# An attention stage ordered by a list planner for five engines, instead of a hand-written slot table for TensorE

## The chip, the cores and the metric

The kernel runs on one core of a Trainium2 chip. The metric is the device time of one execution in microseconds (us). Three executions of the kernel before gave 1341.52, 1343.77 and 1346.31 us; the median is 1343.77.

Five engines work side by side, each through its own instructions in order: TensorE (PE, with its weight loads as PEld), VectorE (DVE), ScalarE (ACT), GpSimd (POOL) and SyncE (SP), which here only issues DMAs.

## The reference

Causal attention over blocks of 64 tokens, and behind it a bilinear feed-forward network (FFN). Eight batches of eight heads, 576 tokens, head size 64; FFN from 512 to 1536 and back to 512, everything in float32.

```python
scores = scale * np.matmul(q, k.transpose(0, 1, 3, 2))        # (8, 8, 576, 576)
mask = block_i >= block_j                                     # blocks of 64 tokens
scores = np.where(mask, scores, -1000000000.0)
scores = scores - np.max(scores, axis=-1, keepdims=True)
attn = np.exp(scores)
attn = attn / (np.sum(attn, axis=-1, keepdims=True) + 1e-09)
x = np.matmul(attn, v)                                        # then heads side by side: (4608, 512)
out = (x @ w_a) * (x @ w_b) @ w_out                           # w_a, w_b: (512, 1536), w_out: (1536, 512)
```

## The kernel before

The 64 heads are taken as 32 pairs, four pairs to a batch. The 12 blocks of 128 FFN columns are cut in two: the first pass computes four of them (F1 = 4) while attention runs, and the two later passes, after attention, compute the other eight. float32 products are made of three products of split halves (hi·hi, hi·lo, lo·hi); the first six pairs (NATIVE) do their scores in plain float32 instead.

For one pair the attention stage does this, on the engines named:

- **Scores** (PE, L384): five tiles of 128 queries, called by their number: tile 3 (512 keys), the side tile 4 (128 keys: the first and the last block of queries), tile 1 (320 keys), then tile 2 (448) and tile 0 (192). Each head has its own PSUM bank; the pool `ps_sc` holds six banks, `ps_mm` two.
- **Maxima** (DVE, `nm`, L389), with memsets for the mask (L395, L407, L408); `nb` joins the maxima of tile 3 and the side tile.
- **Exponentials** (ACT, `e`, L392), and the sums of rows with them; `rc` (DVE) is one over the sums.
- **Normalization** (POOL, L439): every `e` times its `rc`, in place, ten instructions.
- **Transposition** (DVE, L453 and L458): 32x32 blocks of `e` into the buffer `bl`, and then sixteen DMAs from SP (L463, `at<-bl`) which carry the 4x4 block matrix to its transposed places in `at`. There is one `at` (ATB = 1) and one `bl`.
- **Values** (PE, L477, `av`): 60 matmuls of `v` with `at`. They need all sixteen DMAs, and the next pair's sixteen DMAs must wait for them, since `at` is single.
- **x**: ACT copies `av` to `xf`, splits it to `xh` (ACT) and `xl` (POOL), and issues the DMA `xd<-xf` from its own queue.

The first pass of the FFN runs in between on PE (L223, products of 12 matmuls with 288 columns each). After the first product of a block, ACT copies it out (`a`, L247); DVE multiplies the second with it (`hf`, L249); ACT and POOL split that into `hh` and `hl`; the third product (`pso`) is copied by ACT to `ob` and stored by SP. Its weights come from HBM as 64-bit floats and are converted by DVE and ACT (`convert_w`, 12 parts).

The order of the work is fixed on PE alone. A table, SLOT, is walked once per slot (33 slots); in slot s it takes the steps of the softmax of pair s, the transposition of pair s-1 and the values of pair s-1, and after each step it lets as many matmuls of the first pass run as the column of numbers says:

```python
SLOT = [(*S1, 8), (*T1, 0), (*S1, 8), (*T1, 0), (*T1, 0), (*S1, 8), (*T1, 0), (*T1, 0), (*S1, 8),
        (*T1, 0), (*T1, 0), (*T1, 0), (*T1, 0), (*S1, 9), (*S1, 9), (*S1, 9), (*S1, 13), (V_, -1, 0)]
```

Once the first pass has begun, one slot holds 30 score matmuls, 72 of the first pass on average, and 60 value matmuls. On the other engines the framework's scheduler orders the instructions. `keep` matmuls, on zeros, fill PE in the first slots.

After attention the rest of the first pass (336 matmuls with 288 columns), the conversion of the other weights and the two later passes follow (L685, L731).

Of the kernel before, what the change touches and what calls it, by code (L numbers as in the profile page):

```python
# [8 lines left out]
F32 = mybir.dt.float32  # L9
# [11 lines left out]
CONV_POOL = 1  # L21
CONV_POOL2 = 0
CONV_PER_SLOT = 0.88
CONV0 = 1
HL_DVE = False
MOE_FROM = 10.2
FR = 6
X_EVERY = 48
OB = 3
PQ = lambda nc: nc.sync  # L30
XQ = lambda nc: nc.scalar
PE_ORDER = ["PE"]
WARM = 9
ATB = 1
KEEP = [3, 1, 1, 1, 1]
NATIVE = 6

XFB = 2
MORE = 6
PREF = True  # L40
# [4 lines left out]
LATE = 1  # L45
LO2 = lambda nc: nc.vector
CONVP = [1]*12
TLS = False
BEHIND = 5
NOSYNC = mybir.DependencyInfo(mybir.DependencyClass.NoSync, mybir.DependencyReason.DATA)  # L50
CONV_EVERY = 12
# [3 lines left out]
def attention_then_bilinear_ffn(  # L55
# [46 lines left out]
    ps_mm = psum(ctx, "ps_mm", 2)  # L102
# [111 lines left out]
    marks = []  # L214
    lo_eng = [nc.gpsimd]

    def mm3(ps, sets):

        n = 3 * len(sets)
        i = 0  # L220
        for wh, wl, dh, dl in sets:
            for w_, d_ in ((wh, dh), (wh, dl), (wl, dh)):
                mm = nc.tensor.matmul(ps, w_, d_, start=(i == 0), stop=(i == n - 1))  # L223
                if i == 0 and len(marks) > BEHIND:
                    tc.add_manual_dep(mm.ins, marks[-1 - BEHIND].ins.name, NOSYNC, reason="not ahead of attention")
                i += 1
                yield
# [40 lines left out]
    ps_sc = psum(right, "ps_sc", 6)  # L268
# [14 lines left out]
    SIDE, SIDE_T = 3, 1  # L283
    QB = 32
    NQ = P // QB
    NE = 4
    e_bufs, s_bufs = [], []
    for i in range(NE):
        es = [const.tile([P, ew[t]], F32, name=f"e{i}_{t}") for t in range(NT)]
        for t in range(LAST):  # L290
            nc.gpsimd.memset(es[t][:, nk[t]:], 0.0)
        e_bufs.append((es, const.tile([P, P], F32, name=f"e{i}_s")))
    at_e = [sum(ew[:t]) // P for t in range(NT)]
    NE_ = sum(ew) // P + 1
    bl = const.tile([P, NQ, 2, NE_, QB], F32, name="bl")
    nc.gpsimd.memset(bl[:, :, :, NE_ - 1], 0.0)
# [9 lines left out]
    if WARM:  # L306
        z = const.tile([P, W], F32R, name="z")
# [6 lines left out]
    xs_all = {}  # L314

# [13 lines left out]
    def load_qk(p):  # L329

        b, h, n = pair_of(p)
        take(p, "k", S, kT[b, h:h + 2].rearrange("h d s -> (h d) s"))
        take(p, "q", SQ, qT[b, h:h + 2].rearrange("h d s -> (h d) s"))

    def load_v(p):
        b, h, n = pair_of(p)
        vv = heads[p]["v"] = apool.tile([P, 2, NCH + 1, D], F32, tag="v", name=f"v{n}", bufs=3)
        nc.sync.dma_start(vv, vm[b, h // 2])

    def parts_of(p, tag):  # L340
        return heads[p].pop(f"{tag}r"), *(heads[p][tag].bitcast(F32R)[:, j] for j in (1, 0))

    def split_qk(p):
        if p < NATIVE:
            qq = heads[p]["q"]
# [533 lines left out]
```

## Time and profile before

| | |
|---|---|
| median of three executions | 1343.77 us |
| profiled execution: its own time, its span | 1344.45 us, 1342.7 us |
| mean granted PE clock | 0.917 |
| PE busy | 1170.9 us (87%) |
| DVE busy | 907.5 us (68%) |
| ACT busy | 531.3 us (40%) |
| POOL busy | 344.9 us (26%) |
| first score matmul, last value matmul | 5.7 us, 735.6 us |

In lines of the profile, a group reads "line engine operation out<-in shape xcount"; what stands in square brackets is the time the engine was idle just before, and who released it. In the list of waits the three numbers are the total in us, the number of waits and the longest. In the table of windows each engine has its busy time in us and its instructions in brackets; then come the granted PE clock as a share of full speed, the busy share of the DMA engines, and GB/s. SPq is SP's queue of DMA issues.

### The profile page before, as it was taken

Reading aid. Unit: us, or ns where it says so; the run is one execution under the profiler, and the core shown is the slowest. Engines: PE = TensorE matmul, PEld = TensorE weight load, DVE = VectorE, ACT = ScalarE, POOL = GpSimd, SP = SyncE. Lnnn points to the kernel's source line nnn. Section 1 sums busy time; section 2 is a strip of 40 time slices with the busy share of each in tenths; the row PEclk is TensorE's granted clock in tenths of the full one; section 3 lists DMA queues with packets and bytes.
Section 4 is the critical chain, followed back from the end, with each engine's and each line's share of the span. In section 5 each row is a group of like instructions: output and inputs, shape, how many; then the busy total and the mean of one; then the engine's idle time right before and its main releaser. Section 6 shows DMA issues by size and latency. Waiting matters only on the chain.

```text
span 1342.7 us, 23315 instructions
## 1 busy us (share of the span) xinstructions
PE 1170.9 (87%) x8357; PEld 1103.8 (82%) x8357; DVE 907.5 (68%) x2254; ACT 531.3 (40%) x1390; POOL 344.9 (26%) x537
## 2 busy tenths in 40 slices
PE   6466787878787878787877999999999999999998
PEld 3345687768687867686777999999999999999998
DVE  6978656564656465646564998977887876677664
ACT  3435354444444444444443554433433422122110
POOL 2343544444444444444432002102201200000000
PEclk8676988889888889888888999999999999999999
DMA  5666565555555655565545446446628931442231
GB/s 182 185 178 177 156 181 150 143 153 164 148 143 152 164 148 142 154 166 149 139 127 128 159 128 157 123 114 153 159 82 264 304 100 54 130 142 70 73 94 60
DMA packets 88629, 194.50 MB, mean 145 GB/s; under 512 B 15296, under 2 KB 41920, under 8 KB 88512
## 3 DMA queue, kind: packets, MB, share of 16 engines
q1 hardware_dynamic: 76992, 174.12, 45.3%
q0 software_dynamic: 6912, 9.44, 4.4%
q10 hardware_dynamic: 4608, 9.44, 1.9%
q8 instruction: 66, 1.08, 0.4%
q14 instruction: 51, 0.42, 0.1%
HBM read 87.03 MB, written 47.19 MB: 100 GB/s over the span
## 4 chain that ended last, share of the span: by engine, by line
PE 47%; DVE 19%; issue 10%; ACT 9%; POOL 9%; DMA 3%; SPq 2%; DVEq 0%; POOLq 0%; ACTq 0%
PE pso_z L731 14%; DVE bl L453 9%; PE psv_z L685 7%; PE psx_z L685 7%; PE psw_z L685 7%; ACT e L392 6%; DVE nm L389 6%; POOL e L439 4%; PE psy_z L685 3%; PE s L384 3%; PE ps L223 3%; POOL k L115 3%; PE pso L223 3%; DMA v<-vm 2%; SPq L463 1%
## 5 line engine op out<-in xcount | busy, mean ns | idle before, releaser
L223 PE MATMUL ps<-xh,wab 128*128 128x288 f32 x1024 | 233.7, 315 | 49.3 <-ACT a L247 40.9
L223 PEld LDWEIGHTS ps<-xh,wab 128*128 128x128 f32 x1024 | 178.3, 200 | 62.3 <-ACT a L247 45.4
L731 PE MATMUL pso_z<-h_z,wo 128*128 128x384 f32 x1152 | 203.3, 334 | 0.0
L731 PEld LDWEIGHTS pso_z<-h_z,wo 128*128 128x128 f32 x1152 | 200.0, 188 | 0.4 <-ACT h_z L112 0.3
L223 PE MATMUL pso<-hh,wo 128*128 128x288 f32 x480 | 117.3, 334 | 54.7 <-ACT a L247 49.6
L223 PE MATMUL ps<-xl,wab 128*128 128x288 f32 x512 | 159.3, 311 | 3.4 <-POOL xl L115 3.1
L384 PE MATMUL s<-k,q 64*128 64x512 f32 (+3 forms) x900 | 126.2, 416 | 33.4 <-ACT e L392 27.3
L439 POOL TENSOR_SCALAR e<-e,rc 128x512 f32<-128x512 f32 (+3 forms) x256 | 145.4, 586 | 36.8 <-DVE rc L435 36.8
L389 DVE TENSOR_REDUCE nm<-s 128x1 f32<-128x512 f32 (+4 forms) x320 | 142.4, 475 | 3.4 <-PE s L384 1.4
L384 PEld LDWEIGHTS s<-k,q 64*128 64x128 f32 x900 | 91.9, 234 | 61.2 <-ACT e L392 33.7
L223 PEld LDWEIGHTS pso<-hh,wo 128*128 128x128 f32 x480 | 89.9, 216 | 61.1 <-ACT a L247 52.4
L453 DVE STREAM_TRANSPOSE bl<-e 128x512 f32<-128x512 f32 (+2 forms) x256 | 130.5, 575 | 0.9 <-POOL e L439 0.4
L477 PEld LDWEIGHTS av<-at,v 128*64 128x64 f32 x1920 | 102.0, 149 | 31.4 <-issue 19.0
L477 PE MATMUL av<-at,v 128*64 128x128 f32 (+1 forms) x1920 | 106.3, 274 | 24.0 <-DMA at<-bl 22.6
L392 ACT ACTIVATE e<-s,nm 128x448 f32<-128x448 f32 (+2 forms) x192 | 100.1, 533 | 55.1 <-DVE nm L389 54.6
L794 POOL DMA_DIRECT2D part<-pt x48 | 42.7, 1070 | 299.3 <-ACT pt L793 299.3
L112 ACT CAST h_z<-u_z 128x384 fp32r<-128x384 f32 x96 | 49.3, 514 | 176.2 <-DVE u_z L710 160.3
L685 PE MATMUL psw_z<-xh,wab 128*128 128x384 f32 x384 | 116.2, 338 | 0.0
L458 DVE STREAM_TRANSPOSE bl<-e_s 64x64 f32<-64x64 f32 x128 | 27.2, 230 | 131.7 <-POOL e_s L439 123.1
L685 PE MATMUL psv_z<-xh,wab 128*128 128x384 f32 x384 | 116.1, 337 | 0.0
L685 PE MATMUL psx_z<-xh,wab 128*128 128x384 f32 x384 | 116.0, 338 | 0.0
L223 PEld LDWEIGHTS ps<-xl,wab 128*128 128x128 f32 x512 | 102.7, 201 | 6.4 <-POOL xl L115 5.0
(110 smaller groups left out, 2160.2 us busy)
## 6 DMA issues: line engine op xcount, KB each, us to landing
at<-bl SPq DMA_DIRECT2D x512, 112.0 KB, 2.2
xr<-xd SPq DMA_DIRECT2D x48, 384.0 KB, 4.2
raww<-wab SPq DMA_DIRECT2D x24, 512.0 KB, 4.5
v<-vm SPq DMA_DIRECT2D x32, 320.0 KB, 4.1
xd<-xf ACTq DMA_DIRECT2D x32, 288.0 KB, 2.9
part<-ob SPq DMA_DIRECT2D x64, 144.0 KB, 1.8
part<-pt POOLq DMA_DIRECT2D x48, 192.0 KB, 6.6
pt<-part SPq DMA_DIRECT2D x48, 192.0 KB, 3.3
```

What stands on the lines that cost most here:

```text
L112: nc.scalar.copy(hi, src)
L115: return lo_eng.tensor_tensor(lo, src, f32(hi), op=ALU.subtract)
L223: mm = nc.tensor.matmul(ps, w_, d_, start=(i == 0), stop=(i == n - 1))
L384: mark = nc.tensor.matmul(outs[h], qq[r, q0[t]:q0[t] + P], keys, start=j == 0, stop=j == len(qk) - 1)
L389: nc.vector.tensor_reduce(nm[:, h, t:t + 1], view, axis=AX.X, op=ALU.max, negate=True)
L392: nc.scalar.activation(out, view, AF.Exp, bias=bias, accum_out=sm[:, h, t, :1])
L439: nc.gpsimd.tensor_scalar(ev, ev, rc[:, h, t:t + 1], 1.0, op0=ALU.mult, op1=ALU.mult)
L453: nc.vector.transpose(blocks(h, slice(at_e[t], at_e[t] + ew[t] // P), slice(P)), es[t].rearrange("p (c g q) -> p c g q", g=NQ, q=QB))
L477: mark = nc.tensor.matmul(out[d], v[:, h, c], a[:, qs, h, e_], start=start, stop=stop, skip_group_check=True)
L685: nc.tensor.matmul(ps, wt[:, i, iw], j[:, ix], start=start and kp == 0 and i == 0 and j is xh, stop=kp == KP - 1 and i == 1, skip_group_ch ...
L731: nc.tensor.matmul(ps, wt[:, a, osl], b, start=i == 0, stop=i == 3 * len(fs) - 1)
L794: nc.gpsimd.dma_start(part[o * P:(o + 1) * P, ts], t, accum_op=ALU.add)
```

## The change

The attention stage and the first pass are no longer emitted by the slot table. Every step becomes an `Op` with an engine, a duration and a lag (from the table TOOK), the steps that it depends on, and a key. `plan()` runs a list schedule over PE, DVE, ACT, POOL and SP: whichever engine can start first takes the ready step with the smallest key. The steps are then emitted in that order, and the order holds on all five engines, not on PE alone. The keys are a step's place in its pair plus the pair's base, of 12.0 us for each of the first six pairs and 14.6 for the others; matmuls of the first pass come in groups of four (`mm4`) with the largest key, so they fill what is left.

Beside the order it changes these things:

1. The two heads of a pair share PSUM tiles of two banks, `x` (tiles 3 and 2) and `y` (tiles 4 and 1, then 0). Maxima and mask memsets take both heads in one instruction. `ps_sc` becomes x, y (two banks each) and av (one); `ps_mm` has three banks instead of two.
2. Pairs 0 to 3 (PET = 4) are transposed on PE with an identity matrix (`tp`), ten groups of one to four transposes, and copied by ACT into `at`. They need neither DVE transposes nor the sixteen DMAs.
3. `bl` exists twice; `at` stays single. `v` has two buffers instead of three.
4. `xd<-xf` is issued by SP instead of ACT.
5. The low half of a converted weight (`cl`) is made on POOL instead of DVE, and the conversions start 6.5 us apart by plan.
6. From pair 6 on, the values of pair p-2 are tied to follow the scores of tile 0 of pair p, with key 0.

What follows attention is the same code (MORE is 5 instead of 6, and the rest of the first pass again has 336 matmuls).

**SP, one pair.** These rows are SP's around the sixteen DMAs of one pair in the middle of the stage, before: the DMAs `at<-bl` in one piece, then four stores `part<-ob` of the first pass, the loads of `k`, `q` and `v`, and the next pair's sixteen.

```order
L463 DMA at_0_2078<-bl 32x896 x16
L510 DMA part<-ob_0_2173 128x288
L510 DMA part<-ob_1_2202 128x288
L510 DMA part<-ob_2_2237 128x288
L510 DMA part<-ob_3_2335 128x288
L327 DMA kr_0_2458<-kT 128x576
L327 DMA qr_0_2461<-qT 128x640
L338 DMA v_4_2567<-vm 128x640
L463 DMA at_2_2347<-bl 32x896 x16
```

The same stretch of SP in the change, two pairs:

```order
L402 DMA v_0_4040<-vm 128x640
L397 DMA kr_6_4048<-kT 128x576
L397 DMA qr_6_4052<-qT 128x640
L621 DMA at_0_4125<-bl_133 32x896 x3
L663 DMA xd<-xf_6_4129 128x576
L621 DMA at_0_4125<-bl_133 32x896 x13
L757 DMA part<-ob_0_4288 128x288
L402 DMA v_2_4303<-vm 128x640
L397 DMA kr_0_4308<-kT 128x576
L397 DMA qr_0_4317<-qT 128x640
L757 DMA part<-ob_1_4324 128x288
L621 DMA at_2_4384<-bl_134 32x896 x3
```

The store of `xf` now stands inside the block of sixteen, and in the second pair two of the `ob` stores do as well (rows further on: `x3`, xd, one, ob, one, ob, `x11`).

**PE, around the values of one pair.** Before, the values of a pair (`av`) stand at the end of a slot, behind matmuls of the first pass. These rows are PE's at their end, where the next pair's scores of tile 3 follow (`s`, one PSUM bank for each head; the rows go on in turn, three products each):

```order
L477 MATMUL av_4_6048<-at_4_5872,v_4_5819 64x128 x2
L477 MATMUL av_4_6048<-at_4_5872,v_4_5819 64x64 x2
L477 MATMUL av_4_6049<-at_4_5872,v_4_5819 64x64 x2
L384 MATMUL s_0_0_6096<-k_0_5709,q_0_5712 128x512
L384 MATMUL s_0_1_6097<-k_0_5709,q_0_5712 128x512
```

The end of a pair's values on PE in the change (`x` and `y` are scores of the second pair after it, `pso` the first pass):

```order
L630 MATMUL av_0_4328<-at_0_4125,v_0_4040 64x128 x2
L630 MATMUL av_0_4328<-at_0_4125,v_0_4040 64x64 x2
L482 MATMUL x_6_5_4375<-k_6_4047,q_6_4051 128x448 x6
L482 MATMUL y_6_5_4388<-k_6_4047,q_6_4051 128x192 x6
L234 MATMUL pso_2_4310<-hh_1_2_4082,wo_83 128x288
L234 MATMUL pso_2_4310<-hh_1_3_4200,wo_85 128x288
```

The values of a pair moved to the middle of the second pair after it, beside the scores of its tiles 2 and 0; matmuls of the first pass stand on both sides.

**ACT, in an early pair.** Before, ACT's rows of the exponentials of one early pair end like this, and the copies of `av` and the split of `xf` follow, with a conversion between:

```order
L392 ACTIVATE e_1_107,sm_132<-s_4_1_468,nm_4_462 128x320
L392 ACTIVATE e_0_98,sm_132<-s_4_0_542,nm_4_462 128x192
L392 ACTIVATE e_0_106,sm_132<-s_4_1_543,nm_4_462 128x192
L112 CAST wab_84<-xw_0_729 128x512
L142 ACTIVATE sw_1_841<-sw_1_841,shift 128x512
L487 COPY xf_2_595<-av_2_596 128x512
```

In the change ACT's exponentials of pair 4 stand between the copies of the transposed blocks of pair 3 (`at<-tp`):

```order
L528 ACTIVATE e_1_0_104,sm_137<-y_0_1_825,nm_0_837 128x320
L599 COPY at_6_855<-tp_6_1_0_889 128x3x4x32
L528 ACTIVATE e_1_1_108,sm_137<-y_0_1_825,nm_0_837 128x320
L599 COPY at_6_855<-tp_6_1_1_904 128x3x4x32
L599 COPY at_6_855<-tp_6_0_0_922 128x2x4x32
L599 COPY at_6_855<-tp_6_0_1_926 128x2x4x32
L874 CAST wo_79<-xw_2_898 128x512
```

Ten such copies for each of the pairs 0 to 3 were added on ACT; DVE's twelve transposes of each of these pairs (eight of `e`, four of `e_s`) are gone.

The diff, cut to its core (of TOOK, SLOTS and LAGS only what is spoken of):

```diff
+MM = 3
+MORE = 8 - MM
+PET = 4
+SLOTS = [12.0] * 6 + [14.6] * 26
+CONV_STEP = 6.5
+CONV_LO = True
+LAGS = {"PE": 0.24, "DVE": 0.14, "Activation": 0.17, "Pool": 0.1, "SP": 2.0}
+TOOK = {
...
+    "D": (0.6, 1.7, 0), "none": (0, 0, 0), "X": (0.72, 0.17, 0), "xd": (0.33, 2.5, 0), "H0": (0.338, 0.16, 0),
...
-    ps_sc = psum(right, "ps_sc", 6)
+    ps_sc = psum(right, "ps_sc", 1)
...
-    bl = const.tile([P, NQ, 2, NE_, QB], F32, name="bl")
+    bls = [const.tile([P, NQ, 2, NE_, QB], F32, name=f"bl{i}") for i in range(2)]
...
+    def plan():
+        free = dict.fromkeys(LAGS, 0.0)
+        ready = {e: [] for e in LAGS}
...
+        while any(ready.values()):
+            t, e = min((max(free[e], min(map(since, q))), e) for e, q in ready.items() if q)
+            o = min((o for o in ready[e] if since(o) <= t), key=lambda o: (o.key, o.n))
...
+            free[e] = t + o.took + (SWITCH if e == PE_ and o.mode != mode else 0)
...
+            o.start, o.end = t, free[e] + o.lag
+            out.append(o)
...
+        def bank(x):
+            st[x] = ps_sc.tile([P, 2, 512], F32, tag=x, name=f"{x}{n}_{len(st)}")
+            return st[x]
...
+        add("C3", PE_, lambda: scores(LAST, bank("x")), [("ql", p), ("kl", p), ("e2", p - 1)], 0, at=B0, mode=1, kind=nat + "C3")
+        add("C1", PE_, c1, [("C3", p, -LAGS[PE_]), ("e0", p - 1)], 0.1, mode=1, kind=nat + "C1")
...
+        def top(t, view):
+            nc.vector.tensor_reduce(st["nm"][:, :, t], view, axis=AX.X, op=ALU.max, negate=True)
...
+        def pe_turn(t, h):
+            m = 1 if t == NT else ew[t] // P
+            tp = st["tp", t, h] = ps_mm.tile([P, 512], F32, tag="mm", name=f"tp{n}_{t}_{h}")
+            for c in range(m):
+                nc.tensor.transpose(tp[:, c * P:(c + 1) * P],
+                                    e_s[:, h] if t == NT else es[h][t][:, c * P:(c + 1) * P], ident)
+
+        def place(t, h):
...
+            nc.scalar.copy(new_at()[:, :, h, e0:e0 + m].rearrange("p g c q -> p c g q"),
+                           st["tp", t, h][:, :m * P].rearrange("p (c g q) -> p c g q", g=NQ, q=QB))
+
+        by_pe = p < PET
...
+        def move(i, g):
+            new_at()
+            nc.sync.dma_start(st["at"][QB * g:QB * (g + 1), i], bl[QB * i:QB * (i + 1), g])
+
+        ds = ts if by_pe else [Op("D", SP_, lambda i=i, g=g: move(i, g), [o for o in (got("T", p), got("V", p - 1)) if o],
+                 key=B0 + 23) for i in range(NQ) for g in range(NQ)]
...
+        vs = [("D", p), ("lv", p), ("X", p - 1)]
+        for c in range(NCH):
+            o = add("V", PE_, lambda c=c: values(c), vs, 18 if by_pe else 27, mode=2, kind=f"V{c}")
...
+        if p >= 6:
+            done["V0", p - 2].deps.append((done["C0", p], -LAGS[PE_]))
+            for c in range(NCH):
+                done[f"V{c}", p - 2].key = 0
+        v0.frees = add("X", ACT_, evac, [("V", p), ("S1", p - 2), ("xd", p - 2)], 30)
+        add("xd", SP_, lambda: nc.sync.dma_start(xd[hp * P:(hp + 1) * P, b * S:(b + 1) * S], st["xf"]),
+            [("X", p)], 31)
...
-    S1, T1 = (S_, 0), (T_, -1)
-    SLOT = [(*S1, 8), (*T1, 0), (*S1, 8), (*T1, 0), (*T1, 0), (*S1, 8), (*T1, 0), (*T1, 0), (*S1, 8),
-            (*T1, 0), (*T1, 0), (*T1, 0), (*T1, 0), (*S1, 9), (*S1, 9), (*S1, 9), (*S1, 13), (V_, -1, 0)]
...
+    with tc.manual_schedule(engines={getattr(mybir.EngineType, e) for e in LAGS}):
+        for o in plan():
+            o.fn()
```

639 lines of the change are left out of this document (407 added, 232 removed), and 18 rows, old and new, of the table TOOK.

## The prediction

> **What bounds the kernel now.** I read the page first for the granted PE clock, then the table of windows for the stages.
>
> ```profile
> span 1342.7 us, 23315 instructions
> PEclk8676988889888889888888999999999999999999
> ```
> ```profile
> 93.50:114.70 21.20, 12.99 (x90) 9.25 (x88) 18.59 (x46) 10.21 (x30) 7.29 (x10) 0.67 0.45 112
> 407.50:430.40 22.90, 19.21 (x166) 17.64 (x165) 12.91 (x42) 10.15 (x32) 10.40 (x16) 0.85 0.51 136
> 136.00:735.90 599.90, 486.78 (x4361) 446.12 (x4357) 337.36 (x1063) 265.31 (x839) 255.81 (x403) 0.88 0.56 151
> 736.00:1342.70 606.70, 600.97 (x3504) 598.73 (x3503) 464.42 (x904) 208.04 (x382) 42.74 (x48) 1.00 0.46 131
> 407.70:411.60 3.90, 0.30 (x3) 0.07 (x1) 2.00 (x10) 1.73 (x6) 0.00 (x0) 0.94 0.62 144
> 411.70:416.50 4.80, 4.80 (x22) 4.23 (x23) 2.64 (x9) 2.55 (x10) 0.80 (x1) 0.50 0.77 181
> ```
>
> Three stages are seen. From 736 us on, PE is busy for 600.97 of 606.70 us at full clock: the code behind attention, which the change leaves alone. From 136 to 736 us runs the steady attention, and no engine is full: PE 81%, clock 0.88, DVE 56%, POOL 43%. Up to 136 us the early pairs run beside the weight conversion, and there DVE is the full engine (18.59 of 21.20 us).
>
> One steady slot from the timeline, in order of time, shows what PE loses:
>
> ```profile
> 399.95 2.98 PE L477 MATMUL av<-at,v 128*64 128x128 f32 x60
> 402.87 1.74 PE L384 MATMUL s<-k,q 64*128 64x512 f32 x18
> 404.54 0.41 PE L223 MATMUL ps<-xh,wab 128*128 128x288 f32 x1
> 407.45 10.05 SPq L463 DMA_DIRECT2D at<-bl  x16
> 407.71 0.29 PE L223 MATMUL ps<-xh,wab 128*128 128x288 f32 x1
> 411.66 0.61 PE L223 MATMUL ps<-xh,wab 128*128 128x288 f32 x1 [3.65 <-ACT a L247]
> 413.64 2.08 PE L384 MATMUL s<-k,q 64*128 64x448 f32 x12
> ```
> ```profile
> ACT e L392 <- DVE nb L412: 138.9, 30, 5.9
> PE pso L223 <- ACT a L247: 49.6, 12, 4.8
> PE ps L223 <- ACT a L247: 40.9, 13, 3.7
> ```
>
> PE does the values, the scores and 24 matmuls of the first pass, and then stands for 3.65 us: both banks of `ps_mm` are full, and the copy `a` that would free one stands on ACT behind exponentials, which wait for `nb` on DVE. The granted clock is 0.50 in the 4.80 us behind that gap, so that the wait is paid twice. It comes in nearly every slot: 25 such waits are listed, and `nb` held ACT back 30 times.
>
> What a slot's work on PE costs without this: 24 matmuls start from 404.54 to 407.71, 23 steps of 0.138 us, so 72 take 9.9; values 2.98; the first three score tiles 1.74; the other two took 2.08 at half clock, so 1.04. The sum is 15.7 us. The slot as it is comes from the values of pair 4 and of pair 31, on PE:
>
> ```profile
> 135.02 2.98 PE L477 MATMUL av<-at,v 128*64 128x128 f32 x60
> 730.44 5.36 PE L477 MATMUL av<-at,v 128*64 128x128 f32 x60 [6.86 <-DMA at<-bl]
> 48.89 4.82 PE L477 MATMUL av<-at,v 128*64 128x128 f32 x60 [12.48 <-DMA at<-bl]
> ```
>
> (730.44 - 135.02) / 27 = 22.05 us. The span is therefore 135.02 to the values of pair 4, 27 slots of 22.05, 5.36 for the last values, and 606.9 behind them; its sum is 1342.7. My forecast changes the first two terms.
>
> **The steady slot after the change.** The planner lets ACT's copies go first (key -1), and with three banks in `ps_mm` PE may run one product further ahead. The 3.65 us and the slow clock behind them should go, and the order keeps each engine's rows in the sequence in which their inputs come. What is late next is a loop the slot table had slack for: one `at`. The values of a pair need its sixteen DMAs landed; the next pair's sixteen wait for these values. In the loop stand:
>
> ```profile
> DMA to landing us min/median/max: 2.1/2.2/4.1
> 400.94 0.39 SPq L327 DMA_DIRECT2D kr<-kT  x1
> 401.43 0.40 SPq L327 DMA_DIRECT2D qr<-qT  x1
> SPq L510 <- ACT ob L509: 56.9, 54, 5.2
> ```
>
> - Sixteen issues from SP: 10.05 us (the row at 407.45). They were issued at that pace with SP doing nothing else, so no order shortens them.
> - The store of `xf`, which moved from ACT's queue into this block, and of the four `ob` stores of two pairs some three (SP's rows vary): 2.5 issues at the 0.45 us that a load takes (400.94 to 401.43, to 401.88), 1.1 us. Loads of `k`, `q` and `v` stand behind the block and cost nothing.
> - Landing of the last, 2.2 us.
> - The values, 2.98 us at full clock (4.82 when PE is cold, as at 48.89).
> - Two handovers. The sixteen began 0.07 us after DVE's last transpose in this slot (below, 403.32 + 4.06); twice that is 0.15.
> - SP waits in order. An `ob` store waited for its copy 54 times, 1.05 us in the mean; where it stands in the block, everything behind it waits too. Between 0 and 1.6 us (1.5 stores at 1.05); the plan puts a store where its copy is expected to be done, so nearer to 0, and I take 0.4.
>
> The sum is 16.9 us a slot. It lies above PE's 15.7, so PE would stand about 1.2 us before the values; queued behind them on PE are scores of the pair in work and the first pass, and all of that waits too, with room in the slot. The other engines fit beside it by the slot at 407.50, which is the same work or more: DVE 12.91 (less in the change, which joins maxima and masks of two heads: a 512-wide maximum takes 665 ns and a 128-wide one 281, so a joined pair saves the part that does not grow with width, some 0.15 us each), POOL 10.40, ACT 10.15, and the DMA engines 0.51 of 22.90 = 11.7 us. Added `xd` issue, second `bl`, third `ps_mm` bank, fewer `v` buffers: all inside these terms or nothing, since a `v` buffer is freed two slots before its reuse. If POOL were later than the loop allows, the transposes would end late and the sixteen with them; that is the cover that could go.
>
> ```profile
> L389 DVE TENSOR_REDUCE nm<-s 128x1 f32<-128x512 f32 x64 | 40.3, 665 | 1.4 <-PE s L384 1.4
> L389 DVE TENSOR_REDUCE nm<-s 128x1 f32<-128x128 f32 x64 | 15.6, 281 | 0.0
> ```
>
> **The early pairs.** Rows for the first scores of pairs 0 and 4, the transposes of a slot, and ACT's copies from PSUM:
>
> ```profile
> 5.70 1.89 PE L384 MATMUL s<-k,q 64*128 64x512 f32 x12 [0.31 <-POOL q L346]
> 93.53 1.95 PE L384 MATMUL s<-k,q 64*128 64x512 f32 x12
> 402.34 0.97 DVE L458 STREAM_TRANSPOSE bl<-e_s 64x64 f32<-64x64 f32 x4 [4.42 <-POOL e_s L439]
> 403.32 4.06 DVE L453 STREAM_TRANSPOSE bl<-e 128x512 f32<-128x512 f32 x8
> L487 ACT COPY xf<-av x32: 565/586/594, 54.6 to 735.8; 128x512 f32<-128x512 f32 x32
> L488 ACT COPY xf<-av x32: 213/216/219, 55.1 to 736.3; 128x64 f32<-128x64 f32 x32
> L115 DVE TENSOR_TENSOR wab<-xw,wab 128x512 fp32r<-128x512 f32 x8 | 5.7, 716 | 0.9 <-ACT wab L112 0.9
> ```
>
> Four pairs took 93.53 - 5.70 = 87.8 us, 22 each. DVE loses 5.03 us of transposes from its 18.59 and two low halves of 0.72, which leaves 12.1. ACT gains ten copies: between 0.216 (64 wide) and 0.586 (512 wide), by a straight line 2.3 us a head, 4.6 a pair, less some 0.1 each of overlap; 10.21 + 3.6 = 13.8. So ACT binds there, a pair takes 13.8, and pair 4's scores start at 5.7 + 4 * 13.8 = 61. PE's new transposes have no row; they lie between nothing and the 4.82 us of cold values a pair, and PE is busy 12.99 of 21.20 here, so I put them at nothing on the path; with the upper end the pair would take up to 17.5. From pair 4's first scores to its values passed 135.02 - 93.53 = 41.5 us; this pair is transposed by DVE and carried by DMAs as before, so I keep it: values of pair 4 at 102 (93 with 11.5 us a pair, 117 with 17.5).
>
> One rule of the Trainium skill speaks against the transposes: "TensorE: Matmul & The Clock Gate", Part 4, says that PE in transpose mode does not count as busy for the clock, so PE would stay cold in pairs 0 to 3. No run here shows it yet. By it the early values stay at 4.82 us, which the upper end above holds.
>
> **The sum.** 102 + 27 * 16.9 + 5.4 + 606.9 = 1170.6. In slots 7 to 10 the first pass has little to give (24, 76, 20 and 56 matmuls by the order), so PE waits long and the values are cold: four times 1.84, 7.4 us. Span 1178; outside the span the profiled execution had 1344.45 - 1342.7 = 1.75 us, and it lay 0.7 above the median: 1179 us.
>
> **The rivals.**
> - *The loop is shorter, and PE's work binds.* Stores fall outside the block and PE stays warm: 10.05 + 2.2 + 2.98 + 0.15 = 15.4, below PE's 15.7. 102 + 27 * 15.7 + 612.3 = 1138, and with the early pairs at 93, 1129. For it: the rows are fixed lengths. Against: `xf`'s store is in every block. I give it 1132, chance 0.15.
> - *The wait before the values is long enough to cost the clock.* The plan books 0.6 for an issue, 1.7 us for landing, where the rows say 0.63 and 2.2, so PE arrives early at the values in every slot. The gap of 3.65 us gave a clock of 0.50; at that clock the values take 4.82, and since they are in the loop the slot grows to 18.7: 27 * 1.84 - 7.4 more, 1221. With the `ob` waits at their upper end, 1253. The Trainium skill's page "TensorE: Matmul & The Clock Gate", section on why this matters, puts the limit at a gap of about 3 us; the gap of 3.65 us agrees, and by it the 1.2 us expected here would cost nothing. Chance 0.22.
> - *Slower than before.* SP is one queue in order, and `xf`'s and `ob`'s stores now stand among the sixteen. If ACT is late with a copy, SP stands, `at` is late, and PE stands before the values with everything behind them, which makes ACT's next copies late too. It decides where the block is longer by (1343 - 102 - 612.3 - 1.75) / 27 - 16.9 = 6.3 us in every slot. The longest wait of an `ob` store was 5.2, the mean 1.05: against it. At 7 us a slot, 1362. Chance 0.07.
> - *The change doesn't do what it says*: the new order leaves PE where it was, since some other wait takes the 3.65 us; within 0.3% of 1344. The order of four engines is now fixed, where only PE's was, so a wait can't be filled by a ready instruction. Chance 0.02.
>
> **How the numbers follow.** The loop as summed has 0.54, the shorter one 0.15, the cold one 0.22: all faster, 0.91. Slower 0.07, same 0.02, where 0.3% is about what a measurement of this kernel tells from no change. The time is that of the likeliest, 1179 (its own range 1150 to 1205, from 0.0 to 1.0 us of SP waits and the early pairs' ends). The range reaches down past the shorter loop with quick early pairs (1129), and up past the cold one with late stores (1253): 1120 to 1258.
>
> **What would show it.** Right: values 16 to 17.5 us apart, with "DMA at<-bl" as what PE waits for before `av`; the sixteen on SP starting right behind the values; the granted clock near 1 between 150 and 560 us; the waits on `a` gone; the last values near 565 us and 607 us behind them. Wrong: if PE waits for scores or for `a` instead, the order does not hold against the chip's times; if DVE's transposes end after the values, POOL's chain (1/sum, ten normalizations, transposes, the next maxima) is the loop and not `at`; if the early pairs take 17 us or more, ACT or a cold PE is costlier than its rows.

## The result and the profile after

The changed kernel takes 1190.11 us (median of four executions, 1185.94 to 1193.08), the kernel before 1343.26 us beside it. The ratio is 0.8855, with a 95% interval of 0.8824 to 0.8887. The forecast was 1179 us.

The page of the changed kernel, and its table of windows for the early pairs, the steady stage and the code behind attention:

```profile
span 1188.0 us, 23207 instructions
PEclk7999889999999999999899999999999999999999
```
```profile
0.00:84.60 84.60, 62.21 (x490) 40.04 (x490) 60.46 (x126) 59.44 (x175) 53.38 (x84) 0.92 0.46 151
141.00:559.00 418.00, 390.97 (x3890) 360.68 (x3888) 291.31 (x680) 241.36 (x763) 235.78 (x360) 0.98 0.73 197
581.90:1188.00 606.10, 598.19 (x3489) 596.19 (x3487) 462.93 (x900) 206.25 (x375) 42.96 (x48) 1.00 0.46 131
```

In the steady stage PE is busy 391 of 418 us (94%, 81% before) at a clock of 0.98 (0.88 before). The part behind attention is what it was. The early pairs have no full engine: DVE, the busiest beside PE, is busy 60 of 84.6 us.

The values of pair 4 and pair 31 on PE, from the timeline:

```profile
111.29 0.88 PE L630 MATMUL av<-at,v 128*64 128x64 f32 x14
574.44 4.79 PE L630 MATMUL av<-at,v 128*64 128x128 f32 x56 [4.74 <-DMA at<-bl]
```

Pair 4's values start at 111.29 us and end at 114.27 (60 matmuls, of which the row shows the first 14); pair 31's end at 579.23. In between lie 27 slots of 17.22 us, where there were (735.80 - 138.00) / 27 = 22.14 before. So the 154.7 us that the span lost come from two places: 23.7 us up to the values of pair 4, and 27 times 4.92, 132.8, in the slots. The rest behind them grew by 1.9 us (608.8 instead of 606.9).

What PE and SP wait for in the steady stage (141 to 559 us):

```profile
PE x L482 <- ACT e L528: 12.7, 14, 4.1
PE av L630 <- DMA at<-bl: 10.3, 9, 2.1
SPq L621 <- PE av L630: 59.9, 22, 5.7
```

PE's waits for the copy `a`, 90 us before, are gone. The sixteen DMAs are listed as waiting for the values of the pair before in 22 slots, so the loop through the one `at` is closed nearly everywhere. One slot in time, SP first and then PE:

```profile
321.72 2.46 SPq L621 DMA_DIRECT2D at<-bl  x3
324.84 0.33 SPq L663 DMA_DIRECT2D xd<-xf  x1
325.22 0.51 SPq L621 DMA_DIRECT2D at<-bl  x1
325.82 0.53 SPq L757 DMA_DIRECT2D part<-ob  x1
326.40 0.94 SPq L621 DMA_DIRECT2D at<-bl  x1
327.43 0.53 SPq L757 DMA_DIRECT2D part<-ob  x1
328.00 6.88 SPq L621 DMA_DIRECT2D at<-bl  x11
```
```profile
318.82 2.87 PE L630 MATMUL av<-at,v 128*64 128x128 f32 x56 [0.33 <-PE av L630]
337.41 2.87 PE L630 MATMUL av<-at,v 128*64 128x128 f32 x56 [0.93 <-PE av L630]
```

The values end at 321.69 and the first DMA is issued 0.03 us later. With three stores inside, the block ends at 334.88; the last DMA lands 2.4 us behind that, and the next values follow. In the next slot (not shown) only `xd` stood inside.

Over the 27 slots of the timeline the block lasts 12.0 us in the mean, from its first issue to the end of its sixteenth. Its last DMA lands 1.7 us behind that end, and the values end 3.5 us behind the landing: 17.2 us, the whole slot. In 21 of the 27 slots the values end within 3.4 us of the landing, and warm values alone take 2.98. So the loop sets nearly every slot, although PE is listed with only nine waits for `at`: in many others it comes to them at about the time of the landing.

### The profile page after: what moved, and what is told of

It is laid out like the page before. It is cut to its first block, busy times and chain, and to the rows that moved or that the text cites. A ratio compares the mean times of both kernels' runs of the same rounds, so it can differ in the third digit from the quotient of the medians.

```text
span 1188.0 us, 23207 instructions
## 1 busy us (share of the span) xinstructions
PE 1113.1 (94%) x8440; PEld 1051.2 (88%) x8440; DVE 869.0 (73%) x1817; ACT 546.5 (46%) x1430; POOL 377.6 (32%) x553
## 4 chain that ended last, share of the span: by engine, by line
PE 49%; issue 11%; DVE 9%; DMA 8%; SPq 6%; ACT 6%; POOL 4%; DVEq 0%; ACTq 0%; POOLq 0%
PE pso_z L1029 14%; PE psx_z L983 8%; PE psw_z L983 8%; PE psv_z L983 8%; SPq L621 5%; DMA qr<-qT 4%; PE psy_z L983 4%; ACT e L528 3%; PE ps L234 3%; POOL e L571 3%; PE av L630 3%; DVE nm L501 2%; DMA at<-bl 2%; DVE bl L576 2%; PE x L482 1%
## 5 line engine op out<-in xcount | busy, mean ns | idle before, releaser
L234 PE MATMUL ps<-xh,wab 128*128 128x288 f32 x1024 | 212.6, 298 | 0.0
L234 PEld LDWEIGHTS ps<-xh,wab 128*128 128x128 f32 x1024 | 166.3, 189 | 4.6 <-issue 3.4
L576 DVE STREAM_TRANSPOSE bl<-e 128x512 f32<-128x512 f32 (+1 forms) x224 | 116.2, 579 | 48.7 <-DMA at<-bl 31.3
L234 PE MATMUL pso<-hh,wo 128*128 128x288 f32 x480 | 101.6, 300 | 0.0
L482 PE MATMUL x<-k,q 64*128 64x512 f32 (+1 forms) x360 | 63.8, 457 | 32.4 <-ACT e L528 24.8
L234 PEld LDWEIGHTS pso<-hh,wo 128*128 128x128 f32 x480 | 78.4, 189 | 3.3 <-issue 2.2
L528 ACT ACTIVATE e<-y,nm 128x192 f32<-128x192 f32 (+1 forms) x128 | 61.7, 486 | 28.2 <-DVE nm L501 26.0
L501 DVE TENSOR_REDUCE nm<-x 128x2 f32<-128x1024 f32 x64 | 72.9, 1140 | 2.4 <-PE x L482 1.7
L983 PEld LDWEIGHTS psx_z<-xh,wab 128*128 128x128 f32 x384 | 71.0, 187 | 2.8 <-DVE u_z L1001 2.6
L730 POOL TENSOR_TENSOR hl<-hf,hh 128x288 fp32r<-128x288 f32 x56 | 45.8, 818 | 84.2 <-ACT hh L726 81.8
```

What stands on the lines that cost most here:

```text
L482: nc.tensor.matmul(out[:, h], qq[r, q0[t]:q0[t] + P], keys, start=j == 0, stop=j == len(qk) - 1)
L501: nc.vector.tensor_reduce(st["nm"][:, :, t], view, axis=AX.X, op=ALU.max, negate=True)
L528: nc.scalar.activation(out, view, AF.Exp, bias=bias, accum_out=sm[:, h, t, :1])
L576: nc.vector.transpose(dst, es[h][t].rearrange("p (c g q) -> p c g q", g=NQ, q=QB))
L730: nc.gpsimd.tensor_tensor(lo, box2["hf"], f32(hi), op=ALU.subtract)
L983: nc.tensor.matmul(ps, wt[:, i, iw], j[:, ix], start=start and kp == 0 and i == 0 and j is xh, stop=kp == KP - 1 and i == 1, skip_group_ch ...
```

## The experiments

All times are medians; the ratios are to the kernel before, measured beside them. "Pair 4" is where its values start; "slot" is from the end of pair 4's values to the end of pair 31's, over 27. All is read from PE's timeline of each run.

| run | us | ratio (95%) | pair 4 | slot |
|---|---|---|---|---|
| before | 1343.26 | 1 | 135.02 | 22.14 |
| changed | 1190.11 | 0.8855 (0.8824-0.8887) | 111.29 | 17.22 |
| 1 xf's store on ACT | 1181.49 | 0.8798 (0.8770-0.8826) | 112.96 | 16.82 |
| 2 half of the DMAs on ACT | 1204.33 | 0.8964 (0.8938-0.8990) | 113.92 | 17.70 |
| 3 four more DMAs | 1261.88 | 0.9393 (0.9367-0.9419) | 111.28 | 19.91 |
| 4 plan on PE alone | 1306.07 | 0.9723 (0.9692-0.9754) | 142.94 | 20.39 |
| 5 four DMAs for sixteen | 1334.74 | 0.9954 (0.9935-0.9972) | 107.97 | 22.17 |
| 6 low halves on DVE | 1194.49 | 0.8905 (0.8885-0.8924) | 108.61 | 17.50 |
| 7 no transposes on PE | 1205.33 | 0.8987 (0.8964-0.9011) | 114.25 | 17.58 |
| 8 two banks in ps_mm | 1205.73 | 0.8986 (0.8958-0.9015) | 113.34 | 17.77 |
| 9 both stores on ACT | 1204.77 | 0.8967 (0.8940-0.8994) | 113.60 | 17.74 |
| 10 half of the DMAs left out | 1160.46 | 0.8638 (0.8622-0.8655) | 115.24 | 16.07 |
| 11 copies behind exponentials | 1192.96 | 0.8870 (0.8846-0.8894) | 115.70 | 17.21 |
| 12 stores behind the block | 1191.97 | 0.8875 (0.8857-0.8892) | 113.81 | 17.00 |

The changed kernel and runs 1, 2, 3, 9 and 10 have the same plan for the early pairs, and pair 4's values start between 111.28 and 115.24 in them. Differences of less than 4 us in that column say nothing; whether the spread comes from the edits or from chance isn't shown. In runs 5, 6, 7, 8, 11 and 12 the planner ran anew, so that the steady stage came out in another order too.

### Does the loop bind? Runs 3, 1 and 10

Run 3 makes the block longer:

```diff
         def move(i, g):
             new_at()
+            if g == 0:
+                nc.sync.dma_start(dum[QB * i:QB * (i + 1), 1], dum[QB * i:QB * (i + 1), 0])
             nc.sync.dma_start(st["at"][QB * g:QB * (g + 1), i], bl[QB * i:QB * (i + 1), g])
```

> Four more DMAs from SP in every block of sixteen, each of 32 partitions by 512 B of zeros between two spare buffers (ahead of the first, fifth, ninth and thirteenth). Loop theory: every slot is longer by four issues of 0.45-0.63 us, 1.8-2.5 us; 27 slots, 49 to 68 us: 1239-1258. Rival PE: the loop has about 1 us of room a slot, so at most half of it shows, 1190-1215 us. Rival POOL and DVE chain (1/sum, normalizations, transposes): no change.

SP's rows of a slot, of which the first stands ahead of the end of the values (352.91):

```profile
350.49 0.51 SPq L624 DMA_DIRECT2D dum<-dum  x1
352.94 2.17 SPq L625 DMA_DIRECT2D at<-bl  x3
...
360.58 0.59 SPq L624 DMA_DIRECT2D dum<-dum  x1
361.27 2.45 SPq L625 DMA_DIRECT2D at<-bl  x4
```

PE's values in a later slot, a window ahead of their wait and one around them, the steady stage, and PE's wait for `at` in it:

```profile
427.41 4.52 PE L634 MATMUL av<-at,v 128*64 128x128 f32 x56 [2.44 <-DMA at<-bl]
418.00:424.60 6.60, 6.60 (x56) 6.18 (x54) 3.98 (x12) 3.70 (x13) 5.86 (x11) 1.00 0.65 153
427.30:432.00 4.70, 4.59 (x58) 4.56 (x60) 4.41 (x9) 1.55 (x4) 1.43 (x1) 0.64 0.71 252
141.00:559.00 418.00, 360.74 (x3394) 332.92 (x3393) 261.06 (x605) 219.92 (x689) 208.77 (x321) 0.93 0.64 175
PE av L634 <- DMA at<-bl: 43.8, 19, 4.1
```

The slot grew by 2.69 us, and 27 times that is the 72 us that the kernel lost. But only three of the four issues stand in the loop. The first waits for nothing, and SP issues it 1.6 to 5.6 us before the values end, in every slot. Three at some 0.65 us are 1.95 us, and the block is 1.9 us longer in the mean. So the issues in the block are felt at their full length. The other 0.9 us are the values themselves, which end 4.3 us behind the landing instead of 3.5. PE now waits 43.8 us for `at` in 19 waits (10.3 us in 9 in the changed kernel), and in the slot shown the values behind such a wait took 4.52 us instead of 2.87. PE had been busy without a gap at full clock; one wait of 2.44 us, shorter than the gap of about 3 us that the prediction names as the limit, and the clock was 0.64. The time lies 4 us above the range on record: that range had four issues and no slower values. The rows show one thing more: the zeros are 16 KB and the transfers 112 KB, and both were issued at the same 0.6 us.

Run 1 makes the block shorter, by one issue:

```diff
-        add("xd", SP_, lambda: nc.sync.dma_start(xd[...
+        add("xd", SP_, lambda: nc.scalar.dma_start(xd[...
```

> Only the store of xf goes back to ACT's queue, at the place in ACT's order where the plan had it on SP; all else as in the changed kernel (1190 us). Loop theory (one `at`: sixteen issues, landing, values, and SP free for the next sixteen only behind the values): each block of sixteen loses one issue of 0.45 us and SP's waits for xf (about 11 us in 20 waits in the steady stage, 0.4 a slot), so a slot falls from 17.1 to 16.3-16.7 us and the time to 1168-1180 us. Rival PE (PE's own 16.0 busy us a slot and its fixed order bind, the loop only touches them): no change, 1186-1194 us. Rival ACT: ACT's queue now stands for its own store, exponentials come later, slower by up to 10 us.

The slot fell by 0.40 us and the time by 8.6, to 1181.49, both just outside the ranges of the loop theory and clear of "no change": the direction of the loop theory at the price of the one issue (the block is 0.5 us shorter), not of issue and waits. SP's waits moved on to the `ob` stores, 9.0 us where they had been 1.8:

```profile
SPq L757 <- ACT ob L754: 9.0, 18, 1.3
```

This is the best complete version here. It stands 0.7% below the changed kernel by the medians; the two intervals just touch.

Run 10 takes the loop away. It leaves out half of the transfers (the text on record says which), so its time is only a bound:

```diff
-            nc.sync.dma_start(st["at"][QB * g:QB * (g + 1), i], bl[QB * i:QB * (i + 1), g])
+            if g % 2 == 0 or p == PET:
+                nc.sync.dma_start(st["at"][QB * g:QB * (g + 1), i], bl[QB * i:QB * (i + 1), g])
```

> Leaves out half of the transfers at<-bl: from pair 5 on only eight of a pair's sixteen DMAs run (even g), the other half of `at`, now one fixed buffer, keeps old data; the plan is unchanged. The loop is then 5 us shorter and can't bind. What is left shows the next bound: theory PE, 16.0 us a slot (its busy time in the changed kernel: 391 of 418 us, 17.1 us a slot), 1156-1168 us; rival chain (1/sum, POOL, DVE transposes, exponentials) or the fixed order itself, 16.5-17.1 a slot, 1172-1190 us.

```profile
141.00:559.00 418.00, 407.57 (x4116) 380.03 (x4115) 303.37 (x699) 249.86 (x786) 242.54 (x372) 0.98 0.53 154
```

16.07 us a slot, with PE busy for 97.5% of the stretch: PE's own work is what comes next, as that theory said. Over its 27 slots PE is busy for 15.4 us of the 16.07, in the changed kernel for 15.7 of the 17.22. The loop costs (17.22 - 16.07) * 27 = 31 us in the changed kernel.

### Can the block be shortened? Runs 2, 5, 9 and 12

Run 2 splits the issues over two queues:

```diff
-            nc.sync.dma_start(st["at"][QB * g:QB * (g + 1), i], bl[QB * i:QB * (i + 1), g])
+            (nc.sync if g % 2 == 0 else nc.scalar).dma_start(st["at"][QB * g:QB * (g + 1), i], bl[QB * i:QB * (i + 1), g])
```

> Eight of the sixteen DMAs at<-bl of every pair are issued from ACT's queue instead of SP's, at the same places of the plan. Loop theory: the block shrinks from 11-13 us to about 6, so the slot falls to PE's own 16.0-16.4 us and the time by 20 to 30 us, 1160-1170. Rival PE: no change, since PE is busy 93% already, 1186-1194 us. Rival DMA engines (the 0.63 us pace of the sixteen is not SP's but what 16 DMA engines need for 112 KB): the last lands as late as before, the median from issue to landing grows from 2.3 to 5 us or more, and the slot stays; ACT, which now stands through eight issues of some 0.6 us and waits for the values, makes exponentials late, so 1190-1240 us.

The loop theory's number was missed. The time lies in the range of the rival that blamed the DMA engines and ACT, though the landing of 5 us that it named didn't come. The list of DMA issues and SP's waits in the steady stage:

```profile
at<-bl SPq DMA_DIRECT2D x224, 112.0 KB, 3.4
at<-bl ACTq DMA_DIRECT2D x224, 112.0 KB, 3.5
```
```profile
SPq L621 <- DMA at<-bl: 67.8, 37, 5.3
SPq L757 <- ACT ob L754: 41.9, 32, 3.7
```

The stores of `ob` waited 41.9 us for ACT's copies, 1.8 us in the changed kernel: ACT is later now, as that rival said. The landing grew from 2.3 to 3.4 us, and DMAs on SP waited 67.8 us for other DMAs of `at` to land, a wait of 1.1 us in all in the changed kernel. By the trace the DMAs of both queues count their landing on the same eight semaphores in turn, which would make one queue wait for the other without need by the data; that this is the cause is an inference, and no run tests it. The Trainium skill's page "DMA: Bandwidth & Descriptors", section "Issuing engines are not separate DMA queues", says that all issuers share the same sixteen DMA engines and that a second issuer saves only the time of issuing, which is usually small beside the DMA. The longer landing agrees with the first half; that issuing is small doesn't hold here, where sixteen issues took 10 us and a landing 2.3.

Run 9 moves the `ob` stores to ACT as well:

```diff
-        Op("st", SP_, lambda: nc.sync.dma_start(part[...
+        Op("st", SP_, lambda: nc.scalar.dma_start(part[...
```

> Both stores of the attention stage, that of xf and those of ob, are issued from ACT's queue at the places where the plan had them on SP; all else as in the changed kernel. Loop theory: with xf's store alone on ACT the slot went from 17.15 to 16.74 us; some 1.5 ob stores a slot at 0.57 us leave the block as well, so 16.0-16.4 a slot, where PE's own 16.0 takes over, and 1159-1172 us. Rival (the ob stores fill time in which SP would wait for the values anyway, or ACT pays for them): 16.6-16.9 a slot, 1177-1186 us.

Neither came: 1204.77 us. The block now stands in one piece on SP, but SP's DMAs wait inside it for the stores on the other queue to land, which share no data with them:

```profile
SPq L621 <- DMA part<-ob: 16.0, 9, 3.7
SPq L621 <- DMA xd<-xf: 8.4, 7, 2.8
```

In the changed kernel neither wait is listed, in run 1 the second with 0.3 us.

Run 5 makes four large DMAs of the sixteen:

```diff
-            nc.sync.dma_start(st["at"][QB * g:QB * (g + 1), i], bl[QB * i:QB * (i + 1), g])
+            nc.sync.dma_start(st["at"][:, i].rearrange("p h e q -> p (h e q)"),
+                              bl[QB * i:QB * (i + 1)].rearrange("r g h e q -> r g (h e q)"))
```

> The sixteen DMAs at<-bl of a pair become four of 448 KB: a row of `at` is now partition 4r+g instead of 32g+r, so that one DMA reads 32 partitions of bl with four blocks each and fills all 128 partitions; the rows of v from pair 4 on stand in the same order (the sum over keys doesn't mind), and the planner books 0.62 us an issue and 6.0 for landing. Loop theory: issues shrink from 10.05 us to some 2.5, the transfer of 1.8 MB takes 6.8 us at the 270 GB/s that 197 GB/s at a share of 0.73 make, so from the first issue to the last landing 8-9 us instead of 12.3 and a slot of PE's own 16.0-16.3: 1160-1170 us. Rival DMA engines (the pace of the sixteen is what the transfer needs): the last landing 12 us behind the first issue as before, 1186-1195. Rival PE: the loop shrinks, the time doesn't, 1186-1194.

All three were wrong. One slot on SP, the DMA share and rate in it, and the issues:

```profile
416.09 3.15 SPq L621 DMA_DIRECT2D at<-bl  x2
419.29 1.13 SPq L664 DMA_DIRECT2D xd<-xf  x1
420.46 3.45 SPq L621 DMA_DIRECT2D at<-bl  x2
```
```profile
416.10:424.00 7.90, 7.90 (x58) 7.36 (x58) 3.81 (x10) 5.53 (x18) 1.82 (x3) 1.00 0.77 148
```
```profile
at<-bl SPq DMA_DIRECT2D x112, 448.0 KB, 7.5
```

The four issues took 7.8 us with `xd` between them, not 2.5, and all but the first four value matmuls started at 431.14, 15 us behind the first issue. SP was held some 1.6 us by each issue, while 148 GB/s were moved with the DMA engines at 0.77; why an issue takes that long here isn't shown. My 270 GB/s, scaled up from the share, was not reached. That slot was 20.0 us (values ending at 416.06 and 436.02). Besides, four times, every fourth pair, the values stood 28 to 56 us apart; why this plan stalls there is open, so its total says little.

Run 12 keeps the stores on SP and moves them behind the block by the planner's keys:

```diff
-            [("X", p)], 31)
+            [("X", p)], 45)
...
-        Op("st", SP_, lambda: nc.sync.dma_start(part[o * P:(o + 1) * P, tsl], ob["t"]), [c], key=-1)
+        Op("st", SP_, lambda: nc.sync.dma_start(part[o * P:(o + 1) * P, tsl], ob["t"]), [c], key=1e5)
```

> Both stores stay on SP, but the planner's keys put them behind the sixteen: key 45 instead of 31 for that of xf, 1e5 instead of -1 for those of ob, so that nearly every block of sixteen stands in one piece on SP; tiles for a, hf and ob are seven instead of six, since the ob tiles are now held longer. The plan is made anew. Loop theory: 10.05 + 2.2 + 2.98 + 0.15 = 15.4 us, below the 16.07 us a slot that are left with half of the transfers gone, so PE binds at 16.1-16.5 a slot: 1160-1172 us, below the 1181 of xf's store on ACT. Rival (the ob tiles wait for their late stores, and ACT's copies with them; or the new plan falls out otherwise by chance): 16.8-17.4 a slot, 1180-1197 us.

The rival's range was right. The blocks stand in one piece, and PE hardly waits for `at`:

```profile
303.99 11.15 SPq L621 DMA_DIRECT2D at<-bl  x16
...
321.76 10.88 SPq L621 DMA_DIRECT2D at<-bl  x16
```
```profile
PE x L482 <- ACT e L528: 21.1, 15, 2.5
PE av L630 <- DMA at<-bl: 2.0, 2, 1.3
```

Yet a slot is 17.00. The loop itself came out about as summed: sixteen in one piece take 10.1 to 11.8 us, the block lasts 10.8 in the mean, its last DMA lands 1.7 behind it, and warm values take 3.0, 15.5 us in all. But the values end 4.4 us behind the landing. In 22 of the 27 slots PE comes to them only after `at` has landed, and each block starts within 0.1 us of their end (as at 321.76), so PE's lateness is passed on to the next block. PE is busy for 15.7 us of a slot here and waits 1.0 us for exponentials. That reads as two cycles of which each waits for the other, so that a slot is longer than both; no run separates this from the new plan. That `ob` tiles waited for their stores, the rival's reason, isn't seen in the lists of waits.

### What is the order worth, and what the third bank? Runs 4 and 8

Run 4 holds the plan on PE alone:

```diff
-    with tc.manual_schedule(engines={getattr(mybir.EngineType, e) for e in LAGS}):
+    with tc.manual_schedule(engines={mybir.EngineType.PE}):
```

> The plan's order holds on PE alone; ACT, DVE, POOL and SP are ordered by the framework's scheduler again, as in the kernel before. All else (two-bank tiles, three banks of ps_mm, PE transposes, two bl) is as in the changed kernel. Theory order: ACT's copies `a` stand behind exponentials again and PE waits for them 2-4 us a slot: 1240-1300 us. Rival structure (the third bank, joined maxima and PE's own order are what helped): 1180-1200 us, and the waits of PE for `a` stay below 20 us in all.

The time is on the order theory's side, 6 us above its range (1306); the reason is not. PE's waits over the whole span, first of run 4, then of the changed kernel:

```profile
PE x L482 <- ACT e L528: 84.3, 24, 16.4
PE ps L234 <- ACT a L718: 1.7, 1, 1.7
```
```profile
PE x L482 <- ACT e L528: 24.8, 19, 6.5
```

The waits for `a` stay away (1.7 us) although ACT is not ordered. In their place PE waits for exponentials, 60 us more than in the changed kernel, and the clock is 0.89 in the steady stage. Of the 116.5 us of span, 31.7 lie before the end of pair 4's values and 85.5 in the slots. So the wait that I had named as the lost time is gone in run 4 too, and three quarters of the gain are not there. The early gain is gone altogether: the values of pair 4 start at 142.94 us, later than before the change (135.02).

Run 8 takes the third bank away:

```diff
-MM = 3
+MM = 2
```

> Two banks in ps_mm instead of three (MM = 2), the plan made anew for it; the last stage keeps its eight banks. Theory third bank: PE's waits for the copy `a` come back at 1 to 3 us a slot, 1215-1270 us. Rival order alone: the planner puts copies and products where two banks do, 1188-1203 us.

1205.73 us, 2.7 above the range of the rival, and PE's waits for `a` do not come back at all: none is listed. Without the third bank the kernel is 15.6 us slower; how much of that is the new plan isn't known. No run takes away both the order of ACT and the third bank, so either may be enough to keep the waits for `a` away.

### What sets the early pairs? Runs 6, 7 and 11

The values of pairs 0 to 3 came 15.3, 15.8 and 15.6 us apart, not 13.8. Three runs take work from one engine or put it on another.

Run 6:

```diff
-CONV_LO = True
+CONV_LO = False
```

> The low half of the converted weights goes back from POOL to DVE (CONV_LO = False), with the plan made anew for it. Theory POOL chain (in the early pairs the row 1/sum, ten normalizations on POOL, PE transposes, copies, exponentials comes round, and POOL was solid for 10.8 us of 15.5 with low halves of 1.27 us and xl in between): pairs 1 to 3 come 13.5-15 us apart instead of 15.6, pair 4's values start at 102-108 us instead of 111.3, the time falls by 3 to 9 us to 1181-1187. Rival DVE or ACT (their sums bind): 12 times 0.72 us more on DVE, 15.6-17 us apart, values of pair 4 at 111-116, 1190-1195 us.

The pairs came 14.8, 15.8 and 15.2 apart. POOL stood still for 4.0 us behind its normalizations of pair 1 (46.92 to 50.92 us), and the pace hardly changed. So POOL's sum is not the bound.

Run 7:

```diff
-PET = 4
+PET = 0
```

> PET = 0: pairs 0 to 3 are transposed by DVE into bl and carried by the sixteen DMAs like all others. Theory DVE (in the kernel before DVE was the full engine of the early pairs): four times 5.03 us more on a DVE that is busy 60.5 of the first 84.6 us, pairs 18-21 us apart, the values of pair 4 at 120-132 instead of 111.3, 1199-1211 us. Rival recurrence (the chain over POOL is the bound and transposes hang behind it): values of pair 4 within 4 us of 111.3 and 1186-1196 us. The granted clock of the early pairs tells what PE's transposes did to it: by the rule of the Trainium skill that they don't count as busy it should not fall from its 0.92 up to 84.6 us.

```profile
0.00:84.60 84.60, 53.37 (x328) 30.36 (x328) 69.47 (x158) 41.39 (x129) 43.37 (x82) 0.76 0.67 199
```

Pair 4's values start 3 us later, within what the same plan varies by, although DVE is loaded up to 82% and ACT is down to 49%. DVE's sum isn't the bound either, and moving the transposes to PE is not where most of the early gain came from. Of the 15.2 us by which the total rose, 9.6 are the steady slots of the new plan, which are 0.36 longer, and 4.6 lie before the end of pair 4's values, which ran slower.

Run 11:

```diff
-A_KEY = 18
+A_KEY = 22
```

> A_KEY = 22 instead of 18: in the planner's order ACT's copies of the PE-transposed blocks of pairs 0 to 3 come behind the next pair's exponentials instead of between them. Theory order on ACT (in the early pairs the copies wait for POOL's normalizations, and the exponentials queued behind them wait too, so the next 1/sum is late): pairs 1 to 3 come 13.5-14.8 us apart instead of 15.6, pair 4's values start at 103-108 us instead of 111.3. Rival sums (POOL 10.8 us solid and ACT some 13 us a pair bind by themselves): 15.3-16 us apart, pair 4's values at 109-114. The total also depends on how the plan of the steady stage falls out anew, by up to 10 us either way as in the runs before, so the values of pair 4 decide, not the total.

15.6, 18.0 and 15.2 us apart, and pair 4's values later, not earlier, so for the values nothing is gained. The scores did come sooner: pair 4's first at 65.34 us instead of 68.96, lost again behind them.

What is left is the dependency chain of a single pair. It is read from the timeline of the changed kernel and was not tested by a run of its own. One round of it, and the engines' busy time in that round:

```profile
37.82 1.13 PE L482 MATMUL x<-k,q 64*128 64x512 f32 x4
40.19 1.21 DVE L501 TENSOR_REDUCE nm<-x 128x2 f32<-128x1024 f32 x1
43.44 0.16 DVE L518 TENSOR_REDUCE nb<-nm 64x4 f32<-64x8 f32 x1
44.89 0.70 ACT L528 ACTIVATE e<-x,nb 128x512 f32<-128x512 f32 x1
46.59 1.02 PE L482 MATMUL x<-k,q 64*128 64x448 f32 x4
47.98 1.09 DVE L501 TENSOR_REDUCE nm<-x 128x2 f32<-128x896 f32 x1
50.04 0.66 ACT L528 ACTIVATE e<-x,nm 128x448 f32<-128x448 f32 x1
53.12 1.13 PE L482 MATMUL x<-k,q 64*128 64x512 f32 x4
37.82:53.12 15.30, 12.50 (x117) 8.37 (x114) 12.25 (x26) 12.74 (x38) 12.37 (x15) 1.00 0.49 152
```

Since the heads of a pair share the two-bank tile `x`, there is only one `x`: scores of tile 3, their maximum, `nb`, exponentials, scores of tile 2, maximum, exponentials, and only then the next pair's tile 3. The round took 15.3 us. No engine is full in it (ACT, the busiest, has 12.74 us); steps stand behind something else in their engine's order, as the maximum at 40.19 behind the conversion on DVE.

The chain doesn't fix the 15.3 us. With the same single `x`, four rounds up to pair 4's first scores took 14.8 us each in run 11, 14.7 in run 7 (first scores of pair 4 at 65.00 us) and 14.3 in run 8 (63.24), against 15.8 in the changed kernel. Which place in the engines' orders sets the pace remains open.

## Why the prediction was right, and where not

**The slot: right in the mechanism, right in the sum by luck.** 27 slots of 16.9 and 7.4 us for cold values make 463.7; 465.0 were measured. The mechanism stands: run 3 made the loop longer and the slot with it, run 1 shortened it, run 10 took it away. The parts were off both ways. The landing of 2.2 us counts from the start of an issue, and the last issue was already in the 10.05; behind the block it is 1.7. The block took 12.0 us instead of 11.55 (10.05, 1.1 and 0.4), and from the landing to the end of the values it was 3.5 instead of 3.13, since PE came late or the values ran slower in some slots. That made the slot 17.22, not 16.9, 8.7 us over 27 slots; and the 7.4 us for four cold slots, which made up for it, were one cold slot: between 160 and 169 us, at pair 7's values, the clock was 0.51, and slots 7 to 10 came 17.2 us apart in the mean, like the others. PE's own 15.7 us was right (15.7 busy in the changed kernel); where the loop doesn't bind, waits still make the slot 16.07 (run 10). The 0.4 us for SP's waits is what stood before `xd` alone (11.2 us in 21 waits).

**The early pairs: mis-sized, by 9.3 us.** Values of pair 4 at 102 us, measured 111.29, of the 11 us between forecast and median. The step that failed is "ACT binds there, a pair takes 13.8": I took the fullest engine's sum for the pace. ACT was busy for 12.7 us of a round of 15.3, and no engine was full. What sets the pace in its place remains open; the chain through the one `x`, which I had costed at nothing, is a candidate that no run tests. The step behind it, 41.5 us from pair 4's first scores (68.96 now) to its values, measured 42.3.

**The transposes on PE** I put at nothing on the path, and the upper end of cold values did not come: the values of pairs 0 to 3 took 2.98 to 3.15 us, the clock up to 84.6 us was 0.92. The transposes themselves took 4.7 us of PE in the round shown, where PE had room. By the rule of the Trainium skill's page "TensorE: Matmul & The Clock Gate", Part 4, they would not have kept PE warm. Run 7, without them, had a clock of 0.76 there, the other way round; but `keep` matmuls run in both and PE's other work shifts, so that the rule itself isn't decided.

**The waits for `a`** went, as said, but neither reason given is needed by itself: they stay away with ACT unordered (run 4) and with two banks (run 8). What the order of the other four engines buys is above all that exponentials come in time: 60 of the 116.5 us in run 4 are PE's longer waits for them.

**The rivals.** Slower than before: SP's queue did not fall back that far, but run 3 shows that its mechanism is real, with a slot 2.69 us longer for 1.9 us more on SP. Cold values in every slot: no; PE waited 2.1 us at most before the values in the steady stage, and the clock there was 0.98. Its reason was misread as well: the plan's 0.6 and 1.7 us add up to 2.3, and the 2.2 of the rows counts from the start of an issue, so PE was not planned early. But its price is real: run 3 paid 0.9 us of it a slot. The shorter loop: run 12 built it, 15.5 us where 15.4 was said, and the slot was 17.0, since PE came late to it.

## What to carry to other kernels

When a tuned stage is a ring of buffers, look for every loop that closes on a single buffer and add up one turn of it from the rows; where a loop and an engine's own work come within a few per cent of each other, expect a pace slower than either. Before you add up, look whether a duration counts from the start of an issue or from its end. An engine's sum of busy time gives the pace only if that engine is full. When an experiment lengthens a loop, look in the trace whether what was put in stands inside it. And a wait that the profile names may vanish without the gain; what counts is what the engine waits for next.

## What was not expected of the hardware

- From SP a DMA of 16 KB between two places in SBUF was issued at the same pace as one of 112 KB, 0.6 us; loads from HBM of 288 and 320 KB at 0.4 to 0.5 us in the mean. Fewer and larger did not help: four of 448 KB held SP for some 1.6 us each and landed 7.5 us after their issue.
- With two queues in use, DMAs on SP stood until DMAs of the other queue had landed that they share no data with: 24.4 us in 16 waits in run 9.
- A single wait of PE of 2.44 us, behind 6.6 us without a gap at full clock, was followed by a clock of 0.64 in the next 4.7 us (run 3). Values took 4.52 us there instead of 2.87.
- With the same plan for the early pairs, six kernels reached the values of pair 4 between 111.28 and 115.24 us; why they differ isn't shown.
